# A local-attention and two-layer MoE kernel on one core: queries and keys in one load, the mask as a TensorE product, four raw weight buffers

## The chip, the cores and the metric

The kernel runs on one core of a Trainium2 chip. The metric is the device time of one execution in microseconds. The engines spoken of are PE (TensorE, matrix products), DVE (VectorE), ACT (ScalarE), POOL (GpSimd) and SP, which here does nothing but issue DMAs. A change of under 0.2% cannot be told from none for this kernel.

## The reference

The work is an attention over short windows, followed by two feed-forward layers. Inputs are four sequences of 768 positions, eight heads of 64 values, eight memory keys and values per head.

```
for c in range(nc):                       # chunks of 32 queries
    l_start = max(0, c_start - 16); r_end = min(S, c_end + 8)
    k_full = concat([mem_k, k[l_start:r_end]]); v_full likewise
    scores = scale * q_c @ k_full.T
    scores = scores - max(scores); a = exp(scores)
    out[c] = (a / (sum(a) + 1e-09)) @ v_full
x = out.reshape(3072, 512)
x = prelu(x @ w_in1, 0.01) @ w_out1       # 512 -> 2048 -> 512
h = x @ w_in2; x = (h * clip(h + 3, 0, 6) / 6) @ w_out2
```

## The kernel before

**Tiling.** The 3072 tokens are 48 *pairs* (two chunks, 64 queries) and 6 *blocks* of 512 tokens (8 pairs). Everything of layer 0 is done block by block, then everything of layer 1. A block runs through 16 slices f of the 2048 hidden values; for each slice there are 12 products `hidden` (128x512, into the PSUM tile `ph`) and 12 products `output` (into `py`), because each operand is split into a high part and a rest (`xh`, `xl`, `gh`, `gl`) and three of the four cross products are taken. The first pass is block 0 of layer 0; in it the weights of layer 0 are also converted from an 8-byte to a split 4-byte form, one 128x512 tile (layer, f, in or out) at a time. A conversion is a DMA into a `raw` buffer, three ACT instructions (L217, L223, L251) and five DVE instructions (L227, L231, L238, L245, L257).

**Attention of a pair.** PE multiplies queries and keys (`a_scores`, L329, 16 small products), DVE scales and masks them in one instruction (`a_masked`, L338), DVE takes the row maxima (`a_most`, L356), ACT takes the exponential in four instructions, one per head pair, each of which also gives a row sum (`a_exp`, L363), DVE adds 1e-9 to the sums and inverts them (L374, L375), POOL multiplies (`a_norm`, L379), then the weights are transposed: by PE and an ACT copy in pairs 0 to 15 (L397, L402), by twelve DVE transposes in pairs 16 to 47 (L389). PE multiplies with the values (`a_values`, L410), and ACT and DVE split the result into `xh` and `xl` (L425, L431). Block 0's eight pairs come before the first layer product: this is the *opening*. The other pairs are computed while the block before runs; there scores of one pair and values of the pair before share one *visit* of PE.

**What sets the order.** All steps are entered with an engine, a planned length (the table `TIME`), a due time and what they wait for; buffers are counted in `rings`. A planner (`Program.order`) plays this through and fixes the order of the instructions on every engine; on the chip each engine keeps that order and waits on semaphores. Where the planner finds PE with nothing to do in the opening it puts in two small products on a zeroed tile (`keep_warm`, L605). They write the second half of the tile `opening`, whose first half takes PE's transposes.

**Buffers.** There are three `raw` buffers (`NRAW`), two buffers each for queries, keys and values (the first eight pairs use future weight tiles instead), and a pool of three `oo` tiles for the rows of the output.

Of the kernel before, what the change touches and what calls it, by code (L numbers as in the profile page):

```python
# [22 lines left out]
    words=0.67, clip=0.42, shift=0.43, join=0.69, add=0.69, high=0.65, low=0.69, load=0.45,  # L23
    visit=1.2, scores=0.75, masked=0.56, most=0.55, exp=1.65, sums=0.36, norm=0.83, turn=0.6, turned=0.57, turn4=0.95,
# [3 lines left out]
LANDING, RATE = 1.9, 320e3  # L28


BEGIN = 30.0
STEP_FIRST, STEP_MIXED, STEP = 7.0, 6.6, 5.5
PAIR_FIRST = 2.6
# [100 lines left out]
def tile_kernel(  # L134
    ctx: ExitStack,
    tc: tile.TileContext,
    q: bass.AP,
    k: bass.AP,
# [32 lines left out]
    CH, LC, RC = 32, 16, 8  # L171
    CTX = LC + PT + RC
# [6 lines left out]
    NBUF = 2  # L179
    NRAW = 3  # L180
# [14 lines left out]
    q_t = [at.tile([P, HP, PT], F32, tag=f"q{i}", name=f"q{i}") for i in range(NBUF)]  # L195
    k_t = [at.tile([P, HP, W], F32, tag=f"k{i}", name=f"k{i}") for i in range(NBUF)]
    v_t = [at.tile([W, HD], F32, tag=f"v{i}", name=f"v{i}") for i in range(NBUF)]
# [63 lines left out]
    def convert(layer, wanted, after=()):  # L261

        order = [(0, 0)] + [x for f in range(1, NF) for x in ((f, 0), (f - 1, 1))] + [(NF - 1, 1)]
        for f, io in order:
# [11 lines left out]
            c = add("ACT", T["high"], t - 1.6, w_high, key, after=[c] + ([w_ready[layer, f, 0]] if io else []),  # L276
# [8 lines left out]
    def inputs(pr):  # L285
        if pr >= NPB:
            return q_t[pr % NBUF], k_t[pr % NBUF], v_t[pr % NBUF]
        if pr not in in_t:
            in_t[pr] = sb.tile([P, 2 * 2 * 512], F32, tag="w", name=f"in{pr}", bufs=NF)
        t, n, m = in_t[pr], HP * PT, HP * (PT + W)  # L290
        return (
            t[:, :n].rearrange("p (h t) -> p h t", h=HP),
            t[:, n:m].rearrange("p (h w) -> p h w", h=HP),
            t[:W, m:m + HD],
        )

    def load_qk(pr):
        b, p = divmod(pr, PPB)
        qt, kt, _ = inputs(pr)
        nc.sync.dma_start(out=qt.rearrange("p h t -> p (h t)"), in_=q[b, p].rearrange("p h t -> p (h t)"))  # L300
        nc.sync.dma_start(out=kt.rearrange("p h w -> p (h w)"), in_=k[b, p].rearrange("p h w -> p (h w)"))

    def load_v(pr):
        b, p = divmod(pr, PPB)
        nc.sync.dma_start(out=inputs(pr)[2], in_=v[b, p])


    def pa(name, opening=False):
        if opening and "pa" in late:
            return late["pa"]  # L310
        t = ps.tile([P, 2, 512], F32, tag="pa", name=name, bufs=1)
        if opening:
            late["pa"] = t
        return t

    def a_scores(pr):


        qt, kt, _ = inputs(pr)
        if pr < NPB:  # L320
            pt = ps.tile([P, 2, 512], F32, tag="py", name=f"psc{pr}", bufs=2)
        else:
            pt = pa(f"psc{pr}")
        for m in range(HP // 2):
            for j in range(2):
                hp = j * HP // 2 + m
                for e in range(2):
                    r, n = slice(e * D, (e + 1) * D), e ^ j
                    nc.tensor.matmul(  # L329
                        pt[n * PT:(n + 1) * PT, j, m * W:(m + 1) * W], qt[r, hp, :], kt[r, hp, :],  # L330
                        start=True, stop=True, tile_position=(e * D, n * PT),
                    )
        e_t[pr] = p_t[pr] = pt

    def a_masked(pr):
# [57 lines left out]
    def a_turn_pe(pr):  # L393
        e = e_t.pop(pr)
        pt = pa(f"pt{pr}", pr < NPB)
        for hp in range(HP):
            nc.tensor.transpose(pt[:W, 0, hp * P:(hp + 1) * P], e[:, hp, :], ident)  # L397
        aT_t[pr] = pt

    def a_turned(pr):  # L400
        t = at.tile([W, HP, P], F32, tag="aT", name=f"aT{pr}", bufs=2)
        nc.scalar.copy(out=t.rearrange("p h c -> p (h c)"), in_=aT_t[pr][:W, 0, :])  # L402
        aT_t[pr] = t

    def a_values(pr, pt):
        t, vt = aT_t.pop(pr), inputs(pr)[2]
# [9 lines left out]
    def a_values_first(pr):  # L416
        a_values(pr, ps.tile([P, TB], F32, tag="ph", name=f"px{pr}", bufs=2)[:, :HP * PT])
# [15 lines left out]
    x_ready, values_done, pending, opened = {}, [], [], []  # L433
# [10 lines left out]
    def visit(pr):  # L444

        if pr < NP:
            a_scores(pr)
            pt = p_t[pr]
        else:
            pt = pa(f"px{pr}")  # L450
        if pr > NPB:
            a_values(pr - 1, pt[:, 1, HP // 2 * W:HP // 2 * W + HP * PT])

    def attention(pr, t, turned_by_pe, spread):

        blk = pr // NPB
        tag = "py" if blk == 0 else "pa"
# [5 lines left out]
        if blk == 0:  # L463
            qk = vv = [("w", ("in", pr))]
        a = add("SP", 0.9, due(-5), load_qk, pr, takes=qk, nbytes=P * 640 * 4)
        vl = add("SP", 0.45, due(-1), load_v, pr, takes=vv if blk else (), after=[] if blk else [a],
                 nbytes=W * 2048)
        s, e = [(tag, ("s", pr))], [("ye", ("e", pr))]
        if blk == 0:
            before = [values_done[x] for x in [pr - 3] if x >= 0]  # L470
            c = add("PE", T["scores"], due(0), a_scores, pr, after=[a] + before, takes=s)
        else:
            c = visit_step(pr, t, [a], s, qk)
        c = add("DVE", T["masked"], due(1.1), a_masked, pr, after=[c] + set_up, takes=e, frees=s)
        c = add("DVE", T["most"], due(1.7), a_most, pr, after=[c])
        c = add("ACT", T["exp"], due(2.4), a_exp, pr, after=[c])
        c = add("DVE", T["sums"], due(4.2), a_sums, pr, after=[c])
        c = add("POOL", T["norm"], due(4.6), a_norm, pr, after=[c])
        aT = [("aT", pr)]
        if turned_by_pe:  # L480
            p = [("pt" if blk == 0 else "pa", ("t", pr))]
            o = [("pa", "opening")]
            c = add("PE", T["turn"], due(5.6), a_turn_pe, pr, after=[c], takes=p + (o if pr == 0 else []), frees=e)
            c = add("ACT", T["turned"], due(6.3), a_turned, pr, after=[c], takes=aT,
                    frees=p + (o if blk == 0 else []))
# [14 lines left out]
    def visit_step(pr, t, after=(), takes=(), frees=()):  # L500
        if not pending:
            return add("PE", T["scores"], t, visit, pr, after=after, takes=takes, frees=frees)
        p = [*takes] or [("pa", ("s", pr))]
        c = add("PE", T["visit"], t, visit, pr, after=[*pending[:2], *after], takes=p,
                frees=pending[2] + [*frees])
        finish(pr - 1, c, t, p)
# [54 lines left out]
    def output(layer, blk, f, part):  # L561
# [3 lines left out]
        if f == 0 and part == 0:  # L565
            pairs = [
                ps.tile([P, 2, 512], F32, tag="py", name=f"py{layer}_{blk}_{c}", bufs=2) for c in range(2)
            ]
# [213 lines left out]
```

## Time and profile before

| what | value |
|---|---|
| median of 3 runs | 1160.54 us (1160.24 to 1162.18) |
| profiled execution | 1160.1 us |
| its span, first to last instruction | 1158.3 us |
| PE busy | 1140.4 us, 98% |
| DVE busy | 601.8 us, 52% |
| ACT busy | 473.3 us, 41% |
| POOL busy | 42.7 us, 4% |
| moved by DMA | 78.64 MB, 68 GB/s over the span |

The shares are averages over stages that differ. PE's share counts the small products of `keep_warm` as work. How busy DVE is must be read stage by stage: in the page's 40 slices it stands at 8 to 9 tenths in slices 2 to 5, at 5 to 6 tenths up to slice 19, at 7 to 9 tenths around the weights of layer 1, and at 2 to 3 after that.

### The profile page before, as it was taken

The page shows a single profiled execution, that of the slowest core. Times are in us where ns is not written, and L with a number is a line of the kernel's source. Part 1 is how long each engine was busy: PE and PEld are TensorE (multiplying, and loading weights), DVE is VectorE, ACT ScalarE, POOL GpSimd, SP SyncE. Part 2 cuts the span into 40 slices and gives each one's busy share as a digit, 9 for nine tenths or more (in the row PEclk, how much of TensorE's full clock was granted, in tenths as well). Part 3 has the DMA queues.
Part 4 walks back from the last instruction along what each step waited for, and adds up shares of the span by engine and source line. Part 5 has one row for each costly group of instructions (what it writes and reads, how often), then busy time and mean ns, then how long its engine had stood idle before and what let it go on. Part 6 is the DMA issues. An engine that isn't in the chain of part 4 may idle for free.

```text
span 1158.3 us, 16198 instructions
## 1 busy us (share of the span) xinstructions
PE 1140.4 (98%) x6350; PEld 926.1 (80%) x6350; DVE 601.8 (52%) x1303; ACT 473.3 (41%) x1073; POOL 42.7 (4%) x54
## 2 busy tenths in 40 slices
PE   8999999999999999999999999999999999999998
PEld 6777788888888888788888888888888888888886
DVE  5899985555556556555798933223223223222222
ACT  5878853343333333333677623223223223222222
POOL 1100000000000000000000000000000000000000
PEclk9999999999999999999999999999999999999999
DMA  7455531121112112111445401001001000000000
GB/s 237 121 182 183 184 126 55 37 89 40 37 56 74 38 55 74 49 32 73 164 147 181 146 1 64 10 1 64 10 1 64 10 1 28 10 1 28 10 1 37
DMA packets 38573, 78.64 MB, mean 68 GB/s; under 512 B 4193, under 2 KB 16481, under 8 KB 38497
## 3 DMA queue, kind: packets, MB, share of 16 engines
q1 hardware_dynamic: 38496, 77.61, 20.8%
q8 instruction: 50, 0.82, 0.3%
q14 instruction: 27, 0.21, 0.1%
HBM read 65.01 MB, written 12.58 MB: 67 GB/s over the span
## 4 chain that ended last, share of the span: by engine, by line
PE 93%; DVE 4%; DMA 1%; ACT 1%; issue 1%; POOL 0%; ACTq 0%; DVEq 0%; POOLq 0%
PE py L512 44%; PE ph L512 43%; PE psc L410 2%; PE psc L329 2%; PE opening L605 1%; DMA raw<-in_moe_w_out_dram 1%; DVE wa L238 1%; DVE w L257 1%; DVE raw L245 1%; DVE wa L231 0%; PE px L410 0%; DVE e L338 0%; ACT aT L402 0%; PE opening L397 0%; DVE wa L227 0%
## 5 line engine op out<-in xcount | busy, mean ns | idle before, releaser
L512 PE MATMUL ph<-xh,w 128*128 128x512 f32 x768 | 252.5, 390 | 0.4 <-ACT xh L425 0.3
L512 PE MATMUL ph<-yh,w 128*128 128x512 f32 x768 | 252.0, 389 | 0.0
L512 PE MATMUL py<-gh,w 128*128 128x512 f32 x768 | 244.7, 398 | 5.5 <-ACT w L251 3.6
L512 PE MATMUL py<-w,gh 128*128 128x512 f32 x768 | 236.4, 389 | 0.0
L540 DVE SCALAR_TENSOR_TENSOR ph<-g,ph 128x512 f32<-128x512 f32 x96 | 66.8, 696 | 281.3 <-ACT g L534 281.2
L534 ACT ACTIVATE g<-ph,three 128x512 f32<-128x512 f32 x96 | 66.2, 690 | 294.0 <-PE ph L512 294.0
L512 PEld LDWEIGHTS py<-gh,w 128*128 128x128 f32 x768 | 140.5, 188 | 39.4 <-ACT w L251 6.2
L512 PEld LDWEIGHTS ph<-xh,w 128*128 128x128 f32 x768 | 143.9, 188 | 31.7 <-DVE w L257 1.7
L512 PEld LDWEIGHTS ph<-yh,w 128*128 128x128 f32 x768 | 144.3, 188 | 29.9
L512 PEld LDWEIGHTS py<-w,gh 128*128 128x128 f32 x768 | 144.2, 188 | 29.8
L512 PE MATMUL py<-gl,w 128*128 128x512 f32 x384 | 150.2, 391 | 0.0
L512 PE MATMUL ph<-xl,w 128*128 128x512 f32 x384 | 149.5, 389 | 0.0
L512 PE MATMUL py<-w,gl 128*128 128x512 f32 x384 | 149.4, 389 | 0.0
L512 PE MATMUL ph<-yl,w 128*128 128x512 f32 x384 | 149.4, 389 | 0.0
L389 DVE STREAM_TRANSPOSE aT<-e 32x128 f32<-32x128 f32 x384 | 116.0, 302 | 37.6 <-POOL e L379 32.2
L531 ACT ACTIVATE ph<-ph 128x512 f32<-128x512 f32 x96 | 55.9, 582 | 193.8 <-PE ph L512 193.5
L556 DVE SCALAR_TENSOR_TENSOR gl<-ph,gh 128x512 fp32r<-128x512 f32 x96 | 66.3, 690 | 53.1 <-ACT gh L547 53.1
L363 ACT ACTIVATE e<-e,mx 128x96 f32<-128x96 f32 x192 | 69.6, 363 | 59.2 <-DVE mx L356 59.1
L512 PEld LDWEIGHTS py<-gl,w 128*128 128x128 f32 x384 | 72.0, 188 | 15.7
L512 PEld LDWEIGHTS ph<-xl,w 128*128 128x128 f32 x384 | 72.1, 188 | 15.3 <-DVE xl L431 0.3
L512 PEld LDWEIGHTS py<-w,gl 128*128 128x128 f32 x384 | 72.0, 188 | 15.0
L512 PEld LDWEIGHTS ph<-yl,w 128*128 128x128 f32 x384 | 72.1, 188 | 14.9
(59 smaller groups left out, 916.6 us busy)
## 6 DMA issues: line engine op xcount, KB each, us to landing
raw<-in_moe_w_in_dram SPq DMA_DIRECT2D x32, 512.0 KB, 3.5
raw<-in_moe_w_out_dram SPq DMA_DIRECT2D x32, 512.0 KB, 3.5
k<-in_k_dram SPq DMA_DIRECT2D x40, 192.0 KB, 3.0
v<-in_v_dram SPq DMA_DIRECT2D x40, 192.0 KB, 2.6
y_dram<-yo SPq DMA_DIRECT2D x24, 256.0 KB, 2.0
yn<-y_dram SPq DMA_DIRECT2D x6, 1024.0 KB, 5.3
out_dram<-oo SPq DMA_DIRECT2D x24, 256.0 KB, 2.1
q<-in_q_dram SPq DMA_DIRECT2D x40, 128.0 KB, 2.7
```

The source lines that it names most:

```text
L238: nc.vector.scalar_tensor_tensor(out=a, in0=hi, scalar=0xC0000000, in1=a, op0=ALU.bitwise_and, op1=ALU.bitwise_or)
L245: nc.vector.tensor_tensor(out=hi, in0=tmp_t.pop(key), in1=lo, op=ALU.add)
L257: nc.vector.tensor_tensor(out=w[:, io, 1, :], in0=a, in1=w[:, io, 0, :].bitcast(F32), op=ALU.subtract)
L329: nc.tensor.matmul(pt[n * PT:(n + 1) * PT, j, m * W:(m + 1) * W], qt[r, hp, :], kt[r, hp, :], start=True, stop=True, tile_position=(e * D, ...
L363: nc.scalar.activation(out=e[:, hp, :], in_=e[:, hp, :], func=AF.Exp, bias=mx[:, hp:hp + 1], accum_out=su[:, hp:hp + 1],)
L389: nc.vector.transpose(out=t[c, :, r], in_=e[r, :, c])
L410: nc.tensor.matmul(pt[e * D:(e + 1) * D, hp * PT:(hp + 1) * PT], vt[:, c], t[:, hp, n * PT:(n + 1) * PT], start=True, stop=True, tile_posi ...
L512: nc.tensor.matmul(dst, a, b, start=first and i == 0, stop=last and i == len(terms) - 1)
L531: nc.scalar.activation(out=ph, in_=ph, func=AF.Prelu, alpha=0.01)
L534: nc.scalar.activation(out=g, in_=ph, func=AF.Relu, bias=three, scale=1.0)
L540: nc.vector.scalar_tensor_tensor(out=ph, in0=g, scalar=6.0, in1=ph, op0=ALU.min, op1=ALU.mult)
L556: nc.vector.scalar_tensor_tensor(out=gl, in0=ph, scalar=1.0 / 6.0, in1=gh.bitcast(F32), op0=ALU.mult, op1=ALU.subtract)
```

## The change

Queries and keys are laid out side by side and come in one DMA of 128x640 where two came before; for pairs 8 to 47 there is one buffer of them and one of values, where there were two. In pairs 1 to 10 and 13 to 15 (`barred_by_pe`) two bf16 products of a class matrix and a bar matrix put -1e30 into PSUM where a score is not allowed, and the scores accumulate on top. In these pairs DVE's scale-and-mask step is gone; the maxima are taken from PSUM, in two halves, and POOL scales them; ACT's exponential reads PSUM directly. In pairs 2, 4 and 6 (`SHIFTED`) DVE instead subtracts the maxima (two halves), ACT takes one exponential over the whole tile, and DVE adds it up. In all pairs the adding of 1e-9 goes from DVE to POOL. Score tiles are single PSUM banks (`pa0`, `pa1`, `py`) where they were tiles of two banks, `keep_warm` has a bank of its own in the opening, and in pairs 0, 11, 12 and 16 to 47 `a_masked` takes two instructions of half the size. There are four `raw` buffers, and layer 1's output rows use them too (`oo` is gone). The planner has new lengths and due times.

```diff
-LANDING, RATE = 1.9, 320e3
-BEGIN = 30.0
+LANDING, RATE = 2.1, 290e3
+BEGIN = 31.0
-PAIR_FIRST = 2.6
+PAIR_FIRST = 2.1
+SHIFTED = (2, 4, 6)
...
-    NRAW = 3
+    NRAW = 4
...
-    rings = dict(w=NF, raw=NRAW, wa=2, ye=4, aT=2, gh=2, gl=2, x=2, py=2, ph=2, pa=1, pt=1, qk=NBUF, v=NBUF, yn=1, oo=NRAW)
+    rings = dict(w=NF, raw=NRAW, wa=2, ye=4, aT=2, gh=2, gl=2, x=2, py=4, ph=2, pa0=1, pa1=1, qk=1, v=1, yn=1)
...
-            c = add("ACT", T["high"], t - 1.6, w_high, key, after=[c] + ([w_ready[layer, f, 0]] if io else []),
+            c = add("ACT", T["high"], t - 1.6, w_high, key, after=[c, loaded[NPB - 1]] + ([w_ready[layer, f, 0]] if io else []),
...
     def load_qk(pr):
-        nc.sync.dma_start(out=qt.rearrange("p h t -> p (h t)"), in_=q[b, p].rearrange("p h t -> p (h t)"))
-        nc.sync.dma_start(out=kt.rearrange("p h w -> p (h w)"), in_=k[b, p].rearrange("p h w -> p (h w)"))
+        nc.sync.dma_start(out=inputs(pr)[0], in_=qk[divmod(pr, PPB)])
...
+    def barred_by_pe(pr):
+        return pr < 2 * NPB and 0 < pr % PPB < PPB - 1
...
+        more = barred_by_pe(pr)
+        if more:
+            for j in range(2):
+                nc.tensor.matmul(
+                    pt[j][:, :HP // 2 * W], cls, barred.rearrange("p m w -> p (m w)"),
+                    start=True, stop=False, skip_group_check=True,
+                )
...
     def a_most(pr):
+        if barred_by_pe(pr):
+            for j in range(2):
+                nc.vector.tensor_reduce(
+                    out=mx[:, j * HP // 2:(j + 1) * HP // 2],
+                    in_=p_t[pr][j][:, :HP // 2 * W].rearrange("p (m w) -> p m w", w=W),
+                    axis=AX.X, op=ALU.max, negate=True,
+                )
...
+    def a_scaled(pr):
+        mx = m_t[pr]
+        nc.gpsimd.tensor_scalar_mul(mx, mx, SCALE)
...
+    def a_shift(pr):
+        for j in range(2):
+            nc.vector.scalar_tensor_tensor(
+                out=e[:, h, :],
+                in0=p_t[pr][j][:, :HP // 2 * W].rearrange("p (m w) -> p m w", w=W),
+                scalar=SCALE,
+                in1=mx[:, h].unsqueeze(2).to_broadcast([P, HP // 2, W]),
...
+    def a_exp_all(pr):
+        nc.scalar.activation(out=e, in_=e, func=AF.Exp)
...
+    def a_add_up(pr):
+        nc.vector.reduce_sum(out=su, in_=e_t[pr], axis=AX.X)
...
     def a_sums(pr):
-        nc.vector.tensor_scalar_add(su, su, 1e-9)
+        nc.gpsimd.tensor_scalar_add(su, su, 1e-9)
...
         else:
-            t = late["pool"].tile([P, DM], F32, tag="oo", name=f"oo{blk}_{c}", bufs=3)
+            t = sb.tile([P, 512, 2], U32, tag="raw", name=f"oo{blk}_{c}", bufs=NRAW)
...
     def keep_warm():
-        t = pa("opening", True)
+        if "warm" not in late:
+            late["warm"] = bank("pa1", "warm")
```

**The order on SP in the opening** (raw0_0_0 is the first weight tile, in4 to in7 are the inputs of pairs 4 to 7). Before:

```order
L305 DMA in4_159<-in_v_dram 96x512
L300 DMA q0_71<-in_q_dram 128x256
L301 DMA k0_73<-in_k_dram 128x384
L305 DMA in5_185<-in_v_dram 96x512
L211 DMA raw0_0_0_275<-in_moe_w_in_dram 128x1024
```

and now:

```order
L297 DMA in6_135<-in_qk_dram 128x640
L297 DMA in7_141<-in_qk_dram 128x640
L300 DMA in0_96<-in_v_dram 96x512
L211 DMA raw0_0_0_156<-in_moe_w_in_dram 128x1024
L300 DMA in1_105<-in_v_dram 96x512
L211 DMA raw0_1_0_180<-in_moe_w_in_dram 128x1024
```

The first weight tile moved from the 25th DMA to the 10th: all eight loads of queries and keys, and one of values, stand ahead of it.

**The order on DVE in the opening**, from the rest `xl` of pair 2 to that of pair 3 (psc are scores, mx maxima, su row sums, wa and raw belong to a conversion). Before:

```order
L431 TENSOR_TENSOR xl_289<-px_365,xh_288 128x4x64
L245 ISA raw_0_0_275<-raw_0_0_275,wa_0_0_361 128x512x2
L374 TENSOR_SCALAR su_424<-su_424 128x4
L375 RECIPROCAL su_424<-su_424 128x4
L338 SCALAR_TENSOR_TENSOR e_457<-psc_439,masks 128x384
L431 TENSOR_TENSOR xl_289<-px_429,xh_288 128x4x64
```

and now:

```order
L474 TENSOR_TENSOR xl_312<-px_386,xh_311 128x4x64
L418 RECIPROCAL su_417<-su_417 128x4
L231 TENSOR_SCALAR wa_1_0_395<-wa_1_0_395 128x512
L238 SCALAR_TENSOR_TENSOR wa_1_0_395<-raw_1_0_180,wa_1_0_395 128x512
L245 ISA raw_1_0_180<-raw_1_0_180,wa_1_0_395 128x512x2
L356 TENSOR_REDUCE mx_481<-psc_0_463 128x2
L356 TENSOR_REDUCE mx_481<-psc_1_464 128x2
L474 TENSOR_TENSOR xl_312<-px_444,xh_311 128x4x64
```

Between the first and the last `xl` of the opening 14 conversion instructions stood on DVE before, and 23 stand there now.

**The order on PE in the second pass**, around the visit of pair 21 (aT and v belong to the values of pair 20). Before:

```order
L512 MATMUL ph_1_9_2283<-xh_741,w_9_1236 128x512
L329 MATMUL psc_2301<-k_74,q_72 64x96 x8
L410 MATMUL psc_2301<-aT_2265,v_75 64x64 x8
L512 MATMUL py_1_0_1883<-gh_1_8_2269,w_8_1174 128x512 x2
L512 MATMUL py_1_0_1883<-gl_1_8_2290,w_8_1174 128x512
```

and now:

```order
L567 MATMUL py_1_0_1935<-gl_1_8_2354,w_8_1179 128x512
L567 MATMUL py_1_1_1936<-gh_1_8_2329,w_8_1179 128x512 x2
L567 MATMUL py_1_1_1936<-gl_1_8_2354,w_8_1179 128x512
L326 MATMUL psc_0_2374<-qk_now 64x96 x2
L326 MATMUL psc_1_2375<-qk_now 64x96 x2
L326 MATMUL psc_0_2374<-qk_now 64x96 x2
L326 MATMUL psc_1_2375<-qk_now 64x96 x2
L453 MATMUL psc_1_2375<-aT_2331,v_now 64x64 x8
L567 MATMUL py_1_2_1937<-gh_1_8_2329,w_8_1179 128x512 x2
```

The visit moved from ahead of the 12 output products of slice 8 to the middle of them, six products later.

## Rows read from the trace of the kernel before

**Rows 1.** Busy time by stage: stretch and length, engines busy, granted clock, DMA share, GB/s

```profile
0.00:16.30 16.30, 14.38 (x157) 10.52 (x157) 5.39 (x21) 6.64 (x27) 3.18 (x9) 1.00 0.88 251
16.30:41.46 25.16, 19.89 (x295) 15.27 (x291) 17.80 (x43) 19.05 (x65) 4.13 (x5) 1.00 0.48 151
41.46:150.46 109.00, 103.34 (x661) 78.87 (x661) 104.93 (x210) 90.06 (x206) 8.48 (x8) 1.00 0.58 180
150.46:1153.30 1002.84, 1002.76 (x5244) 821.45 (x5243) 473.02 (x1032) 356.95 (x778) 26.90 (x32) 1.00 0.15 50
```

**Rows 2.** Groups by line on DVE, 16.30 to 41.46 us: busy, mean ns, idle before

```profile
L338 DVE SCALAR_TENSOR_TENSOR e<-psc,masks 128x384 f32<-128x384 f32 x6 | 3.3, 553 | 2.9 <-PE psc L329 2.9
L431 DVE TENSOR_TENSOR xl<-px,xh 128x256 fp32r<-128x256 f32 x8 | 3.3, 409 | 2.6 <-ACT xh L425 2.4
...
L227 DVE TENSOR_SCALAR wa<-wa 128x512 f32<-128x512 f32 x3 | 1.3, 446 | 2.2 <-ACT wa L217 2.2
```

**Rows 3.** Groups by line on DVE, 41.46 to 150.46 us

```profile
L245 DVE CUSTOM_DVE_ANT_0 raw<-raw,wa 128x1024 uint16<-128x1024 uint16 x29 | 23.7, 818 | 1.9
L257 DVE TENSOR_TENSOR w<-raw,w 128x512 fp32r<-128x512 f32 x30 | 20.4, 679 | 0.0
L238 DVE SCALAR_TENSOR_TENSOR wa<-raw,wa 128x512 uint32<-128x512 uint32 x29 | 19.9, 685 | 0.3
...
L338 DVE SCALAR_TENSOR_TENSOR e<-psc,masks 128x384 f32<-128x384 f32 x9 | 5.0, 552 | 0.6 <-PE psc L410 0.5
L356 DVE TENSOR_REDUCE mx<-e 128x4 f32<-128x384 f32 x9 | 4.9, 544 | 0.0
...
L375 DVE RECIPROCAL su<-su 128x4 f32<-128x4 f32 x8 | 1.4, 178 | 0.3
L374 DVE TENSOR_SCALAR su<-su 128x4 f32<-128x4 f32 x8 | 1.3, 164 | 0.0
```

**Rows 4.** The chain that ended last, in order of time: start, length, what

```profile
1.05 5.93 PE opening L605 x28
...
141.84 0.44 PE pt L397 x4
...
146.39 0.49 PE psc L329 x16
146.88 0.61 PE psc L410 x16
147.50 2.96 PE py L512 x12
150.46 2.72 PE ph L512 x12
```

**Rows 5.** Instructions on ACT in the opening: one in order of time, one by line

```profile
21.10 0.68 ACT L217 ACTIVATE wa<-raw 128x512 f32<-128x512 f32 x1
...
L363 ACT ACTIVATE e<-e,mx 128x96 f32<-128x96 f32 x20 | 7.2, 362 | 0.1
```

**Rows 6.** POOL and DVE side by side, in order of time; start, length

```profile
139.94 1.09 POOL L379 TENSOR_TENSOR e<-e,su 128x384 f32<-128x384 f32 x1 [13.02 <-DVE su L375]
...
140.26 1.31 DVE L245 CUSTOM_DVE_ANT_0 raw<-raw,wa 128x1024 uint16<-128x1024 uint16 x1
```

**Rows 7.** POOL by line, whole span: a step of 128 columns

```profile
masks.py:199 POOL TENSOR_SCALAR_AFFINE_SELECT ident<-ident 128x128 f32<-128x128 f32 x1 | 0.3, 292 | 0.1
```

**Rows 8.** The last copies, in order of time

```profile
1153.26 0.69 DVE L587 COPY oo<-py 128x512 f32<-128x512 f32 x1 [0.67 <-PE py L512]
1154.74 0.58 ACT L589 COPY oo<-py 128x512 f32<-128x512 f32 x1 [1.53 <-DMA out_dram<-oo]
```

**Rows 9.** Second pass: scores and `a_norm` of pair 21, rest `gl` of slice 10

```profile
207.45 0.56 PE L329 MATMUL psc<-k,q 64*64 64x96 f32 x16
...
213.38 0.83 POOL L379 TENSOR_TENSOR e<-e,su 128x384 f32<-128x384 f32 x1 [11.35 <-DVE su L375]
...
217.09 0.69 DVE L554 TENSOR_TENSOR gl<-ph,gh 128x512 fp32r<-128x512 f32 x1
```

More of the change, by code (lines that the diff above doesn't have):

```diff
@@ L22 @@
 TIME = dict(
-    words=0.67, clip=0.42, shift=0.43, join=0.69, add=0.69, high=0.65, low=0.69, load=0.45,
-    visit=1.2, scores=0.75, masked=0.56, most=0.55, exp=1.65, sums=0.36, norm=0.83, turn=0.6, turned=0.57, turn4=0.95,
+    words=0.67, clip=0.42, shift=0.43, join=0.69, add=0.69, high=0.65, low=0.69, load=0.47,
+    visit=1.2, scores=0.75, masked=0.56, most=0.55, exp=1.65, exp_all=0.52, small=0.15, inverse=0.18, norm=0.83, turn=0.6, turned=0.57, turn4=0.95,
     values=0.85, xh=0.4, xl=0.45, half=1.36, act=0.58, six=0.69, gh=0.6, gl=0.69, done=0.66, warm=0.22,
@@ L171, in tile_kernel @@
     CH, LC, RC = 32, 16, 8
+    PT, D = 2 * CH, P // 2
+    HP = HD // P
     CTX = LC + PT + RC
@@ L303, in load_v @@
     def load_v(pr):
[L304 to L314, printed above, removed]
-    def a_scores(pr):
[L319 to L323, printed above, removed]
+        nc.sync.dma_start(out=inputs(pr)[3], in_=v[divmod(pr, PPB)])
@@ L464, in attention @@
             qk = vv = [("w", ("in", pr))]
[L465 to L468, printed above, removed]
+        hold = [] if blk == 0 else [scored[-3]] if pr == NPB else loaded[-1:]
+        a = add("SP", T["load"], due(-5), load_qk, pr, after=hold, takes=qk, nbytes=P * 640 * 4)
+        loaded.append(a)
@@ L469, in attention @@
+        vl = add("SP", T["load"], due(0), load_v, pr, takes=vv if blk else (), after=[a], nbytes=W * 2048)
+        s = [("py" if blk == 0 else f"pa{j}", ("s", pr, j)) for j in range(2)]
+        e = [("ye", ("e", pr))]
+        direct = barred_by_pe(pr)
         if blk == 0:
             before = [values_done[x] for x in [pr - 3] if x >= 0]
-            c = add("PE", T["scores"], due(0), a_scores, pr, after=[a] + before, takes=s)
+            c = add("PE", T["scores"] + 0.3 * direct, due(0), a_scores, pr, after=[a] + before + set_up, takes=s)
@@ L478, in attention @@
+        c = add("POOL", T["small"], due(4.1), a_sums, pr, after=[c])
+        c = add("DVE", T["inverse"], due(4.3), a_inverse, pr, after=[c])
         c = add("POOL", T["norm"], due(4.6), a_norm, pr, after=[c])
@@ L480, in attention @@
         if turned_by_pe:
[L481 to L485, printed above, removed]
+            p = [("pa0", ("t", pr))]
+            c = add("PE", T["turn"], due(5.6), a_turn_pe, pr, after=[c], takes=p, frees=e)
+            c = add("ACT", T["turned"], due(6.3), a_turned, pr, after=[c], takes=aT, frees=p)
             if blk == 0:
@@ L565, in output @@
         if f == 0 and part == 0:
[L566 to L569 removed]
+            acc[layer, blk] = [bank("py", f"py{layer}_{blk}_{c}") for c in range(4)]
         dst = acc[layer, blk]
```

157 lines of the change are left out of this document (95 added, 62 removed).

## The prediction

> **What bounds the kernel now.** I read the busy time by stage first, because the page's shares run over stages with different limits. It shows four stages [rows 1]. From 150.46 to 1153.30 us PE is busy for 1002.76 of 1002.84 us: nothing on another engine can shorten that. From 41.46 (end of the opening's last `xl`) to 150.46 (first product of the second pass) DVE is busy for 104.93 of 109.00 us. From 16.30 (first `xl`) to 41.46 no engine is full: DVE has 17.80 of 25.16, ACT 19.05. Before 16.30 the first pair runs through, behind 28 products that only keep PE busy and take 5.93 us [rows 4], 0.21 each.
>
> Next come the groups by line, for durations and for what ended DVE's idle time. In the opening DVE waited for scores (2.9 us), for `xh` (2.6) and for the first weights (2.2) [rows 2]; ACT's first conversion starts only at 21.10 [rows 5]. In the first pass the largest groups are the conversions [rows 3]. Then the chain of waits, for PE's own needs: 12 products 2.72 us; a visit 0.49 + 0.61, and 2.96 - 2.72 = 0.24 more for the products behind it, 1.34 in all; a transpose 0.44 [rows 4]. Between 41.46 and 150.46 PE has 31 groups of 12 products, 8 visits and 8 transposes: 84.3 + 10.7 + 3.5 = 98.5 us. So PE lost 10.5 of the 109.0, and DVE only 4.1. Last, the end: ACT's last copy waited 1.53 us for a store to free an `oo` buffer [rows 8].
>
> One rule of counting. DVE's instructions overlap: the fourteen groups of 41.46 to 150.46 sum to 117.5 us (the seven used here are [rows 3]), but cover 104.93. I count an instruction as 0.893 of its duration.
>
> **The opening.** The order puts 32 instead of 28 idle products ahead of the first scores: 4 x 0.21 = 0.85 us, so the first `xl` comes at 17.15 instead of 16.30. For the rest of that first pair I let POOL's two extra hand-overs cancel against the copy that no longer waits behind idle products. From there DVE has, in its new order up to the last `xl`: ten tensor-scalar steps of conversions at 0.446, five joins at 0.685, four L245 at 0.818, four L257 at 0.679 [rows 2, 3], 14 half-size steps (ten maxima, four shifts), two sums at 0.544, five inversions at 0.178, eight `xl` at 0.409. No row shows a half-size step or a maximum from PSUM. Its bounds are half of 0.55 (0.275) and the whole 0.55. L431 with 256 elements takes 0.409 and L356 with 384 takes 0.544, which is 0.34 for 192 on a straight line; I take that. Sum 4.5 + 3.4 + 3.3 + 2.7 + 4.8 + 1.1 + 0.9 + 3.3 = 24.0, times 0.893 = 21.4 us. Without any wait the last `xl` ends at 38.5. ACT hides behind this: it gets four more conversion instructions of 0.68 (2.7) and loses two pairs' worth of eight exponentials (2.9, and their reads) [rows 5], so it stays near 19 us.
>
> Waits: the three named above shrink. The first weight tile stands tenth on SP. Ahead of it and with it are 8 x 0.328 + 0.197 + 0.524 = 3.34 MB, which at the 251 GB/s of the first stage [rows 1] is in by 13.3 us, ahead of 17.15. Nine more conversion instructions stand between the pairs' steps and fill what were gaps. What comes late next is a sum or a maximum that POOL passes on. POOL's small step (128x4) has no row: its bounds are nothing and 0.83, the whole `a_norm` of 128x384 [rows 9]; I take 0.3, by the step of 128 columns [rows 7]. I allow 0.65 us of waits in all. The last `xl` then ends at 39.2 instead of 41.46: **-2.3 us**. Bounds: no waits and half-steps of 0.275 give 37.7 (-3.8); all of DVE's old 7.36 us of idle time kept, 45.9 (+4.4), and half-steps of 0.55 another 2.6 on that.
>
> **The first pass.** More of the conversions now lie before it: on DVE two fewer of L227, L231, L238 and L257 and one fewer L245 fall in the stretch, 5.3 us. Six pairs (8, 9, 10, 13, 14, 15) lose L338, 3.3 us; eight lose L374, 1.3 us; two half-size steps for one whole add 0.13 nine times, 1.2. Together -8.7, times 0.893 = -7.8: DVE's need falls from 104.9 to about 97.1. PE gets two mask products in each of six visits. Nearest rows are 0.21 for an idle product of 256 columns and 2.72 / 12 = 0.227 for one of 512 [rows 4]; bounds 0.04 and 0.227 each. I take 0.1 for 192 columns, 1.2 us, so PE needs 99.7. PE becomes the bound, with DVE close under it; I allow 1.8 us of waits where a weight part still comes late: 101.5 instead of 109.0, **-7.5 us**. Bounds: PE alone with free mask products, 98.5 and 0.5 (-10.0); DVE with its old 4.1 us of idle time and 0.69 us more for each of 14 small POOL steps, 110.9 (+1.9). The fourth `raw` buffer has no term of its own: it is what lets loads and conversions run as far ahead as the order has them, and without it the 4.1 stays.
>
> **The rest and the end.** In the stretch in which PE is full no product is added or removed: 0, with 2 us either way for visits that now write two single banks. The second half-size step of each later pair (0.13 us) and the single input buffer lie under DVE at 473 of 1003 us: a load goes out right after the visit that frees it, a visit comes every 12 us. At the end the last copy needs no store to be done, so it can start at 1153.26 with DVE's, not 1154.74 [rows 8]. Its store then waits behind the other on SP, some 0.4 us: **-1.0 us**, bounds -1.5 and 0.
>
> Sum: -2.3 - 7.5 - 1.0 = -10.8. The profiled execution took 1160.1 us, 0.44 under the median, so 1149.3 in its terms and **1149.7 us** against the median of 1160.54.
>
> **Rivals.** *POOL and DVE in each other's way.* When a POOL step and L245 ran together, the POOL step took 1.09 instead of 0.83 and L245, which has two inputs as L238 has, 1.31 where that takes 0.685 [rows 3, 6, 9]. The change adds 15 small POOL steps to the opening and 14 to the first pass, and in these DVE waits for 18 of their results (16 inversions, two shifts) with everything queued behind. If each is held up by 0.69 less the 0.16 that L374 took, that is 9.5 us, 1159.2; if half of it, 4.8 us, 1154.5. Against it: the planned order leaves some other step between most sums and their inversion.
>
> The Trainium skill, "SBUF — State Buffer", section "Who interferes with whom", says that GpSimd and VectorE share a port pair as an exclusive lock, so that a VectorE step with two SBUF inputs and a GpSimd step that reads SBUF block each other for the whole instruction. The two steps of rows 6 agree. Applied to every new step it gives the 1159.2, and it speaks for moving nothing small to POOL.
>
> *The opening is overfilled.* The nine conversion instructions come on top of DVE's old waits instead of into them: last `xl` at 45.9, sum -4.1, 1156.4. For it: DVE keeps its order and stands still behind any late step.
>
> *The weights don't come early.* If the first tile still lands so that ACT starts at 21.10, DVE is 4 us later: 1153.7.
>
> *Slower, in passes two to five.* There 32 pairs have a chain in which POOL's sum is new: scores, maxima, exponential, sum, inversion, `a_norm`, nine transposes, then `gl`, which PE wants. Before, from scores at 207.45 to the end of `gl` at 217.78 it took 10.33 us [rows 9]. The visit is now six products later, so that from scores to the first use of that `gl` PE has 1.34 + 1.36 + 3 x 2.72 + 2 x 0.23 = 11.3 us of other work: about 1.0 of room, 1.4 as another `gl` no longer stands in the chain. POOL's step eats the room and then stops PE 32 times. It cancels the gain at 10.8 / 32 = 0.34 beyond the room, so if the step costs 1.75 us more than before; at 2.0 the result is 1149.7 + 19.2 = 1168.9. Against it: even the whole `a_norm` takes only 0.83.
>
> **How the numbers follow.** Forecast 64% (its own range 1146.0 to 1153.0), POOL and DVE 16%, overfilled opening 10%, late weights 4%, slower 6%. The lower end is the sum of the three terms' low bounds, -15.3: 1145.2. The upper end, 1156.5, takes in the overfilled opening, the late weights and the first rival up to two thirds of its price; what lies above is under 2 in 10. Under 0.2% (2.3 us) this kernel's change can't be told from none. Faster: all but the slower rival and the full price of the first, 91%; same 3%; slower 6%.
>
> **What would show it.** Right: ACT's first conversion near 17 us, the opening's last `xl` ending near 39.2, the second pass starting near 140.7, PE's own idle time in the first pass under 3 us, the last copy of ACT starting with DVE's. Wrong: DVE's inversions idle on POOL for more than 5 us in total up to 140 us; idle time of PE in the second to fifth pass; a last `xl` after 41.

## The result, and the profile after

The changed kernel takes 1149.95 us (median of 4 runs, 1149.60 to 1150.69), the kernel before 1161.24 on the same chip (4 runs): ratio 0.9904, 95% interval 0.9887 to 0.9921. The profiled execution has a span of 1148.9 us against 1158.3.

| point, us | before | forecast | after |
|---|---|---|---|
| first `xl` starts | 16.30 | 17.15 | 16.64 |
| opening's last `xl` ends | 41.46 | 39.2 | 39.97 |
| second pass starts | 150.46 | 140.7 | 142.42 |
| ACT's last copy starts | 1154.74 | (at PE's end) | 1145.20, at PE's end |
| span | 1158.3 | 1147.5 | 1148.9 |

Busy time by stage, as [rows 1]; the last stretch runs to PE's end:

```profile
0.00:16.64 16.64, 15.20 (x162) 11.44 (x166) 4.95 (x22) 6.19 (x22) 5.32 (x22) 1.00 0.89 281
16.64:39.97 23.33, 20.04 (x307) 14.85 (x299) 22.75 (x53) 19.31 (x55) 8.62 (x15) 1.00 0.53 163
39.97:142.42 102.45, 101.18 (x670) 79.91 (x671) 96.19 (x194) 83.87 (x200) 14.19 (x22) 1.00 0.60 189
142.42:1145.18 1002.76, 1002.74 (x5244) 821.21 (x5243) 472.65 (x1032) 357.36 (x777) 34.93 (x64) 1.00 0.15 50
```

The third number of busy time is DVE's. In the opening it is now 22.75 of 23.33 us, where 7 us were idle; in the first pass it fell from 104.93 to 96.19. PE stays full behind that. By stage the time changes by +0.3 (first pair), -1.8 (to the last `xl`), -6.6 (first pass), 0, and -1.3 us behind PE's end.

DVE by line in the opening, first `xl` to last, to be read against [rows 2]:

```profile
L238 DVE SCALAR_TENSOR_TENSOR wa<-raw,wa 128x512 uint32<-128x512 uint32 x5 | 3.9, 780 | 0.1
L356 DVE TENSOR_REDUCE mx<-psc 128x2 f32<-128x192 f32 x11 | 3.4, 346 | 0.0
L257 DVE TENSOR_TENSOR w<-raw,w 128x512 fp32r<-128x512 f32 x4 | 3.3, 834 | 0.0
L474 DVE TENSOR_TENSOR xl<-px,xh 128x256 fp32r<-128x256 f32 x8 | 3.3, 414 | 2.0 <-ACT xh L468 2.0
L245 DVE CUSTOM_DVE_ANT_0 raw<-raw,wa 128x1024 uint16<-128x1024 uint16 x4 | 3.3, 820 | 0.3
L227 DVE TENSOR_SCALAR wa<-wa 128x512 f32<-128x512 f32 x5 | 2.7, 537 | 0.0
L231 DVE TENSOR_SCALAR wa<-wa 128x512 uint32<-128x512 uint32 x5 | 2.6, 521 | 0.1
```

and in the first pass, against [rows 3]:

```profile
L238 DVE SCALAR_TENSOR_TENSOR wa<-raw,wa 128x512 uint32<-128x512 uint32 x27 | 20.6, 763 | 0.5
L245 DVE CUSTOM_DVE_ANT_0 raw<-raw,wa 128x1024 uint16<-128x1024 uint16 x28 | 19.2, 686 | 0.6
L257 DVE TENSOR_TENSOR w<-raw,w 128x512 fp32r<-128x512 f32 x27 | 19.0, 705 | 0.2 <-ACT w L251 0.2
```

The waits for scores and for the first weights in [rows 2] are gone. The 2.0 us for `xh` end at 16.64 and so lie ahead of this stretch; in [rows 2], too, 2.42 of the 2.6 us end at 16.30 and are no part of DVE's 7.36 us of idle time there. But the joins L238 take 780 ns where the prediction counted 685, L257 834 for 679, L227 537 for 446: DVE is full partly because its steps became longer. What ran beside a long one is seen here, as in [rows 6]; DVE, then POOL:

```profile
24.84 1.20 DVE L238 SCALAR_TENSOR_TENSOR wa<-raw,wa 128x512 uint32<-128x512 uint32 x1
```

```profile
24.67 0.83 POOL L422 TENSOR_TENSOR e<-e,su 128x384 f32<-128x384 f32 x1 [0.28 <-DVE su L418]
```

In the first pass PE needs 98.5 us and six times the two mask products, of which one pair reads:

```profile
97.13 0.18 PE psc L317 x2
```

That makes 99.6 us, and the pass takes 102.45. Of the 2.85 lost, 0.7 is the first `xl`, and two breaks at 117 and 131 us cost about 1.0 each. The chain through the second:

```profile
129.63 0.79 POOL su L414
...
130.54 0.41 DVE wa L231
...
130.97 1.20 DVE wa L238
132.17 0.61 DVE w L257
...
132.82 0.73 PE py L567 x2
```

POOL's small step, 0.23 alone, took 0.79 here, and the join beside the `a_norm` that follows took 1.20; `w` is late by that, and PE waits. In each break PE first waits 0.3 us for `a_norm` itself, ahead of the transposes. The end, as [rows 8]:

```profile
1144.52 0.69 DVE L640 COPY oo<-py 128x512 f32<-128x512 f32 x1 [0.67 <-PE py L567]
...
1145.20 0.58 ACT L642 COPY oo<-py 128x512 f32<-128x512 f32 x1 [0.77 <-PE py L567]
```

No copy waits for a store any more. DVE's last copy also starts 0.68 us ahead of PE's end, since each accumulator has a bank of its own.

### The profile page after: what moved, and what is told of

It reads as the page before. It is cut to its first block, busy times and chain, and to the rows that moved or that the text cites. A ratio compares the mean times of both kernels' runs of the same rounds, so it can differ in the third digit from the quotient of the medians.

```text
span 1148.9 us, 16191 instructions
## 1 busy us (share of the span) xinstructions
PE 1139.2 (99%) x6370; PEld 927.4 (81%) x6370; DVE 596.6 (52%) x1299; ACT 467.3 (41%) x1052; POOL 63.1 (5%) x123
## 4 chain that ended last, share of the span: by engine, by line
PE 96%; DVE 2%; ACT 1%; POOL 0%; issue 0%; DVEq 0%; POOLq 0%
PE py L567 46%; PE ph L567 45%; PE psc L453 2%; PE psc L326 2%; PE warm L659 1%; DVE wa L238 1%; DVE w L257 0%; ACT e L402 0%; PE pt L440 0%; DVE raw L245 0%; DVE wa L231 0%; DVE xl L474 0%; DVE mx L356 0%; DVE wa L227 0%; POOL su L414 0%
## 5 line engine op out<-in xcount | busy, mean ns | idle before, releaser
L609 DVE TENSOR_TENSOR gl<-ph,gh 128x512 fp32r<-128x512 f32 x96 | 66.2, 690 | 59.6 <-ACT gh L600 58.5
```

The costliest lines, as they stand in the source:

```text
L609: nc.vector.tensor_sub(out=gl, in0=ph, in1=gh.bitcast(F32))
```

## The experiments

All times are of one profiled execution beside the median of its runs. PE is full from the second pass on in each (1002.8 us), so the start of that pass is PE's end less this. The column that compares best is the time from the first `xl` to the second pass. The profiled run is not always near the median of its kernel: it is 2.3 us above it in small_dve, 1.9 in norm_act, 1.7 in mask_dve, and 1.4 below it in two_loads. An edit that the planner sees can also give a new order, so only small_twice is sure to change one part and nothing else.

| kernel | first `xl` | last `xl` ends | second pass | first `xl` to second pass | span | median |
|---|---|---|---|---|---|---|
| before | 16.30 | 41.46 | 150.46 | 134.16 | 1158.3 | 1161.24 |
| changed | 16.64 | 39.97 | 142.42 | 125.78 | 1148.9 | 1149.95 |
| changed, again | 16.45 | 39.80 | 142.21 | 125.76 | 1148.7 | 1149.72 |
| raw3 | 15.97 | 39.32 | 147.59 | 131.62 | 1154.9 | 1157.03 |
| before_raw4 | 16.20 | 41.00 | 151.51 | 135.31 | 1158.7 | 1160.49 |
| mask_dve | 15.90 | 37.38 | 148.58 | 132.68 | 1155.5 | 1155.65 |
| small_dve | 16.53 | 40.91 | 145.46 | 128.93 | 1152.0 | 1151.80 |
| small_twice | 16.31 | 40.30 | 144.82 | 128.51 | 1151.3 | 1153.26 |
| two_loads | 13.70 | 38.55 | 142.86 | 129.16 | 1149.4 | 1152.53 |
| norm_act | 15.41 | 38.75 | 145.35 | 129.94 | 1151.8 | 1152.05 |
| norm_dve_open | 16.22 | 37.18 | 144.32 | 128.10 | 1151.1 | 1151.98 |
| idle_priced | 14.03 | 37.30 | 139.83 | 125.80 | 1146.3 | 1148.14 |
| idle_noshift | 13.71 | 37.95 | 139.06 | 125.35 | 1145.6 | 1147.31 |
| idle_costs | 13.79 | 39.66 | 142.67 | 128.88 | 1149.2 | 1150.62 |

The first theory was the prediction's: fewer and earlier DVE steps in the first pass, with the fourth raw buffer as what lets them run ahead. The rivals: POOL's new steps and DVE hinder each other enough to eat part of it; the buffers alone are the gain. What the new planned lengths and due times bring by themselves was not run.

**Three raw buffers.**

```
-    NRAW = 4
+    NRAW = 3
```

> The changed kernel with three raw buffers instead of four. The theory of the prediction: the fourth buffer is what lets loads and conversions run ahead, and it lets the last copy start without a store. Without it the first pass goes from 102.45 us to 104 to 106.5 (4.1 us of DVE waits come back, part of it hidden since PE needs 99.7), and the time from PE's last product to the end of the span from 3.72 us back to about 5.1; span 1152 to 1154. Rival A, the ring does not matter to the first pass: only the tail moves, span 1150.3. Rival B, the ring is the main part of the gain: first pass near 109, span 1157 or more.

The opening keeps its length; the first pass takes 108.3 us, more than the theory's 106.5 and near rival B's 109. DVE has 97 us of work in it, as with four: little is added, it waits. The chain up to PE's longest two breaks shows for what:

```profile
77.49 1.25 DVE w L257
78.74 0.02 issue
78.75 4.96 DMA raw<-in_moe_w_in_dram
83.71 0.02 issue
83.73 0.67 ACT wa L217
...
89.02 0.43 DVE wa L231
89.45 0.60 DVE w L257
```

```profile
90.10 0.73 PE L567 MATMUL ph<-xh,w 128*128 128x512 f32 x2 [1.22 <-DVE w L257]
...
94.84 0.64 PE L440 MATMUL pt<-ident,e 128*96 128x128 f32 x4 [2.15 <-POOL e L422]
```

A load goes out when the step that frees its buffer is done, and with three buffers its 4.96 us stand open on the path. The weight part is late, and behind it in DVE's order the maxima of a pair, so that its `a_norm` is late as well. The end has its old wait back:

```profile
1151.28 0.59 ACT L642 COPY oo<-py 128x512 f32<-128x512 f32 x1 [1.65 <-DMA out_dram<-oo]
```

**Four raw buffers, in the kernel before.**

```
-    NBUF = 2
-    NRAW = 3
+    NBUF = 1
+    NRAW = 4
...
```

The lines left out put the output rows into the raw ring too, as in the change.

> The kernel before with only the buffers changed: single input buffers, four raw buffers, and the output rows in the raw ring. Theory: a part of the gain. The first pass loses some of DVE's 4.1 us of waits, 109.0 to 106 or 107; the tail falls by about 1.0; opening 0 to -1; span 1158.3 to about 1154.5. Rival A, the buffers are nearly all of the gain: 1150. Rival B, only the tail moves, since DVE's need of 104.9 in the first pass stays: 1157.3.

Ratio 0.9999 (0.9990 to 1.0008): nothing, less than any theory expected. Its first pass:

```profile
41.00:151.51 110.51, 103.39 (x661) 79.12 (x662) 105.30 (x210) 90.23 (x206) 9.01 (x8) 1.00 0.59 179
```

DVE still has 105.30 us to do, so there is little that earlier loads could gain. The pass even got 1.5 us longer, against 0.4 less in the opening and 0.6 less behind PE's end. The edit also takes away the second input buffers, and what that costs is not separated here from what the ring gives; PE's longest wait (1.79 us, for a copy by ACT at 112 us) is longer than any of the kernel before (0.69). So the fourth buffer with the single input buffers brings nothing in this kernel, while its loss costs the changed one 5.8 us. That the DVE work had to go first agrees with both, but is argued.

**Mask on DVE again.**

```
     def barred_by_pe(pr):
-        return pr < 2 * NPB and 0 < pr % PPB < PPB - 1
+        return False
```

> The changed kernel with the mask added by DVE for every pair again, so without mask products, without POOL's small shift step and without the one-piece exponentials of pairs 2, 4 and 6. Theory: in the first pass DVE gets 6 x 0.62 us back (96.2 to about 99.9 busy) while PE's need falls by 1.1, so both engines have about 99 of work and the pass takes 103 to 105 instead of 102.45; in the opening ACT gets three pairs' eight exponentials back, about 1 us each, and becomes as full as DVE: 0.5 to 2 us longer. Span 1150 to 1153. Rival: PE alone sets the first pass now, so that taking the mask products away gains what they cost, span 1147.5 to 1148.5.

Longer by 6.9 us from the first `xl` to the second pass, where 4.6 at most was expected.

```profile
37.38:148.58 111.20, 101.74 (x660) 80.37 (x661) 104.43 (x208) 87.81 (x204) 11.58 (x16) 0.98 0.58 177
```

DVE is back at 104.43 us in the first pass: the masked sums, and conversions that the new order no longer puts into the opening, which got shorter by 1.85. What PE waits for is `a_norm`, 7.9 us in four waits. The rival (mask products cost more than they spare) is out. About 1.3 of the 6.9 is PE's clock (below); by the medians the loss is 5.7.

**The small steps on DVE.**

```
-        nc.gpsimd.tensor_scalar_mul(mx, mx, SCALE)
+        nc.vector.tensor_scalar_mul(mx, mx, SCALE)
...
-        nc.gpsimd.tensor_scalar_add(su, su, 1e-9)
+        nc.vector.tensor_scalar_add(su, su, 1e-9)
...
```

> The changed kernel with the two small steps (sum plus 1e-9, scaling of the maxima) on DVE instead of POOL, everything else alike. Theory: POOL's small steps cost little and take DVE work away; back on DVE they add 12 x 0.16 us to the DVE-bound opening and 14 x 0.16 to the first pass, where DVE has about 6 us to spare: span 1150 to 1151.5. Rival (POOL and DVE in each other's way): DVE's two-input steps get shorter and the chains through POOL's lengthened sum step (0.79 and 0.81 us at 115.6 and 129.6) go, span 1145 to 1147.4.

Slower by 3.1 us in the profile and 1.85 by the medians, where the rival wanted it 1.5 to 4 us faster: the prediction's first rival is refuted for the small steps. Of the 3.1, 1.05 lie in the opening. In the first pass a drop of the clock follows PE's waits at 36 to 41 us: the first 23 products take 7.02 us there and 5.48 in the changed kernel, so 1.5 is not DVE's work. The 1.6 us left, a gain of having the steps on POOL, are under 0.2%, less than can be told from none for this kernel.

```profile
40.95 7.02 PE ph L567 x23
```

**The small steps done twice.**

```
         nc.gpsimd.tensor_scalar_mul(mx, mx, SCALE)
+        nc.gpsimd.tensor_scalar_mul(mx, mx, 1.0)
...
         nc.gpsimd.tensor_scalar_add(su, su, 1e-9)
+        if pr < 2 * NPB:
+            nc.gpsimd.tensor_scalar_add(su, su, 0.0)
```

> The changed kernel with each of POOL's small steps of the first 16 pairs done twice (the second adds 0 or multiplies by 1; the order is planned as if there were one). It doubles the suspected cost: 29 more steps of 0.23 us alone, up to 0.8 beside DVE. Theory: most of it lies beside DVE's conversions, since some other DVE step is queued between a sum and its inversion only in part; 1 to 3 us longer, span 1150 to 1152. Rival (each small step costs 0.5 us or more on the path that sets the end): 8 to 15 us longer, span 1157 or more.

Longer by 2.7 us from the first `xl` to the second pass, as the theory had it. Of the 29 new steps, five stand ahead of that stretch and 24 in it: 0.11 us each, where the rival wanted 0.5.

**Two loads for queries and keys.**

```
-        nc.sync.dma_start(out=inputs(pr)[0], in_=qk[divmod(pr, PPB)])
+        n, src = HP * PT, qk[divmod(pr, PPB)]
+        nc.sync.dma_start(out=inputs(pr)[0][:, :n], in_=src[:, :n])
+        nc.sync.dma_start(out=inputs(pr)[0][:, n:], in_=src[:, n:])
...
```

> The changed kernel with queries and keys of a pair loaded by two DMAs again (same bytes, same buffer). Theory: the joining of the loads has next to no effect of its own; SP issues eight more in the opening at about 0.4 us each, so values and weights are issued some 3 us later, ahead of their use still: 0 to 0.7 us longer, span 1149 to 1149.6. Rival: the first weights and values come later than DVE wants them, as SP stands between: 2 to 3.5 us longer, span 1151 to 1152.4.

Unclear by stage: the planner, told of the longer issue, put out another order on PE ahead of the first `xl` (13.70), and the stretch behind it lost 3.4 us. The profiled run's span of 1149.4 is the theory's, but the median is 2.6 us over the changed kernel's, against 0.7 at most, and the spans of its other three runs, 1150.6 to 1151.0, come near the rival's 1151. DVE is busy for 21.11 of 24.85 us of this opening (22.75 of 23.33 in the changed kernel): it waits again. What the load itself costs is not separated from the order here.

**`a_norm` of pairs 8 to 15 on ACT.**

```
+        if NPB <= pr < 2 * NPB:
+            for hp in range(HP):
+                nc.scalar.activation(out=e[:, hp, :], in_=e[:, hp, :], func=AF.Identity, scale=su[:, hp:hp + 1])
...
```

> The changed kernel with the product of e and the inverted sums of pairs 8 to 15 on ACT (four steps by head pair) instead of POOL. It takes away POOL's long steps in the first pass, beside which DVE's two-input steps take 1.20 instead of 0.69. Theory: what PE still loses in the first pass (102.45 less a need of 99.7) comes from these meetings, above all the 1.20 at 116.9 and 131.0; DVE's busy time there falls by about 4 us, PE's loss by 1 to 1.5: second pass from 141 to 141.5, span 1147.3 to 1148. Rival: ACT, at 84 of 102 us, gets 8 us more and its copies for the weights come later: span 1149 to 1151.

The theory fell, and the rival's mechanism came: DVE's busy time fell by 2.3 of the 4 us expected, to 93.86, yet the pass takes 106.60.

```profile
38.75:145.35 106.60, 103.58 (x670) 80.89 (x671) 93.86 (x194) 91.65 (x232) 5.74 (x14) 0.98 0.59 181
```

ACT has 91.65 us, its copy for one weight part comes 1.4 us late, and the clock falls behind that wait (some 1.6 us). The profiled run is the slowest here; the other three have spans of 1149.0 to 1150.7, in the rival's range. What a meeting of POOL and DVE costs PE was not had back with ACT's time, and how much of PE's loss in the first pass comes from these meetings stays open.

**`a_norm` of pairs 0 to 7 on DVE.**

```
-        nc.gpsimd.tensor_tensor(out=e, in0=e, in1=su.unsqueeze(2).to_broadcast([P, HP, W]), op=ALU.mult)
+        eng = nc.vector if pr < NPB else nc.gpsimd
+        eng.tensor_tensor(out=e, in0=e, in1=su.unsqueeze(2).to_broadcast([P, HP, W]), op=ALU.mult)
...
```

> The changed kernel with the product of e and the inverted sums of pairs 0 to 7 on DVE instead of POOL (pairs 8 on as before). Between the opening's first and last xl DVE gets five such steps more, about 0.53 us each by the maximum over the same 128x384 (0.54): 2.65 us. Theory (a POOL step and a DVE step block each other, and the longer DVE steps at 22.04, 24.84, 28.80, 32.35 and 35.26, 2.8 us over their usual times in sum, are time that DVE loses): the two cancel, and the stretch takes 23.0 to 23.8 us instead of 23.33, DVE's mean of one step back at 0.69 for the join. Rival: the longer durations are only counted twice, DVE loses little by them, and the stretch takes 25.5 to 26.2; span then 2 to 3 us longer than 1148.9.

Neither stretch came: the planner moved five conversion steps out of the opening, which so took 20.96 us. The steps themselves bear on the question. DVE in this opening:

```profile
L423 DVE TENSOR_TENSOR e<-e,su 128x384 f32<-128x384 f32 x5 | 2.8, 556 | 0.1
L238 DVE SCALAR_TENSOR_TENSOR wa<-raw,wa 128x512 uint32<-128x512 uint32 x4 | 2.8, 688 | 0.1
L245 DVE CUSTOM_DVE_ANT_0 raw<-raw,wa 128x1024 uint16<-128x1024 uint16 x3 | 2.1, 693 | 0.2
L257 DVE TENSOR_TENSOR w<-raw,w 128x512 fp32r<-128x512 f32 x3 | 2.1, 684 | 0.0
L231 DVE TENSOR_SCALAR wa<-wa 128x512 uint32<-128x512 uint32 x4 | 1.7, 427 | 0.1
L227 DVE TENSOR_SCALAR wa<-wa 128x512 f32<-128x512 f32 x4 | 1.7, 419 | 0.0
```

Without POOL's long step beside them they are back at 688, 684 and 419 ns (780, 834, 537 in the changed kernel). Over L238, L257, L227 and L231 that is 5 x 0.09 + 4 x 0.15 + 5 x 0.12 + 5 x 0.09 = 2.1 us, and 4 x 0.13 = 0.5 more with L245. By this estimate the opening of the changed kernel loses 2.6 us to five `a_norm`, nearly the 2.8 us that they take on DVE: the two cancel, as the theory said, though the stretch itself does not show it. To the second pass this kernel is 2.3 us longer, about 1.5 of it by the clock.

**Idle products at their price.**

```
-                        free_at[e] = now + filler[1]
+                        free_at[e] = now + filler[1] * (1 if began else 2)
...
```

Here `began` says that the planner has placed a step that is no idle product.

> The changed kernel, but the program that sets the order counts an idle product ahead of the first scores at twice its cost, near the 0.205 us that the trace shows for each (32 in 6.57 us) where it counted 0.11. So 16 instead of 32 stand ahead of the first scores. Theory: the first pair's chain is one after the other, and the input of pair 0 is there at about 3.7 us, so all of it moves forward by 16 x 0.205 = 3.3 us, the DVE-bound stretch behind it starts that much sooner, and the whole is 2 to 3 us faster (second pass from 142.42 to about 139.5 to 140.5, span 1146 to 1147). Rival A: the products of the first pairs then run at half the rate, as the idle ones do, and give back 1 to 2 us: span 1147.5 to 1148.5. Rival B: the values' input and the first weights land no sooner, so DVE waits what it gains: span 1148.5 to 1149.5.

As the theory had it. The chain up to the first `xl`:

```profile
1.04 3.60 PE warm L660 x16
4.64 0.86 PE psc L327 x16
...
14.03 0.42 DVE xl L475
```

Sixteen idle products instead of 32, scores at 4.64 instead of 7.62, and everything behind comes 2.6 us sooner at unchanged length (125.80 and 125.78). Rival A shows in one place only: these scores take 0.86 us instead of 0.50. The ratio is 0.9894 (0.9880 to 0.9909). By the medians it is 1.8 us faster than the changed kernel, and the two intervals overlap.

**No shift by DVE, on top of idle_priced.**

```
-SHIFTED = (2, 4, 6)
+SHIFTED = ()
```

> idle_priced with no pair shifted by DVE: pairs 2, 4 and 6 get their exponentials from PSUM in four steps on ACT, as 1, 3 and 5 do. DVE, which sets the opening (22.69 of 23.27 us busy), loses 3 x (0.62 + 0.54) = 3.5 us, ACT gets 3 x 0.8 = 2.4 on 19.3. Theory: the stretch from the first to the last xl falls by 0.8 to 1.8 us, to about 22, with both engines near full; span 1144.5 to 1145.5 against 1146.3. Rival: ACT, in its order, becomes what DVE waits for (its copies for the weights stand behind the exponentials), stretch 23 to 25, span 1146.3 to 1148.

```profile
13.71:37.95 24.24, 21.99 (x327) 16.96 (x319) 20.37 (x48) 21.16 (x70) 9.15 (x15) 1.00 0.74 199
37.95:139.06 101.11, 100.40 (x670) 80.06 (x671) 95.96 (x193) 85.07 (x200) 13.61 (x22) 1.00 0.61 190
```

The opening did not get shorter, as the rival said (DVE waits for ACT now), but the first pass did, by 1.4. It is the best kernel here: 1147.31 us, ratio 0.9883 (0.9870 to 0.9897), against 0.9906 (0.9893 to 0.9920) for the changed kernel on the same chip. Against idle_priced the 0.8 us are within the two intervals and stay open.

**More of the planner's costs set to the trace**, on top of idle_priced; six entries of `TIME`:

```
-    ... join=0.69, ... scores=0.75, ... exp=1.65, ... small=0.15, ... norm=0.83, turn=0.6, ...
+    ... join=0.75, ... scores=0.52, ... exp=1.4, ... small=0.35, ... norm=0.95, turn=0.5, ...
```

> idle_priced with more of the order's costs set to what the traces show: scores 0.52 (was 0.75), the exponentials of a pair 1.4 (1.65), POOL's small step 0.35 (0.15), POOL's product 0.95 (0.83), the join 0.75 (0.69), the turn 0.5 (0.6). No instruction is added or taken away. Theory: what PE still loses in the first pass (2.7 us) is order that was planned with wrong lengths, and 0.5 to 1.5 us of it go: span 1144.8 to 1145.8. Rival: these waits come from in-order queues that no cost mends; any new order is as good as the old, within 2 us either way: 1144.5 to 1148.5 without a pattern in the waits.

Neither range held: the median is 2.5 us over that of idle_priced, and the span of 1149.2 lies above even the rival's 1148.5. The opening has 24.04 us of DVE work in 25.87 and the first pass gains nothing. A cost that is right by itself need not make the order better.

**The changed kernel again.**

> The changed kernel itself, once more, beside the others on one chip. It tells how much of the spread is the 32 idle products: they took 6.57 us in the profiled run and 4.97 to 5.89 us in other runs with as many. Theory: the start of the scores moves by as much from run to run, and from the first xl to the second pass the time is the same, 125.8 within 0.3 us. Rival: the stretch behind the first xl varies as much as the start.

The theory held: 125.76 us, and the start carries the spread. The profiled run of the changed kernel was the slowest of its four (1150.69), its idle products the slowest of all.

## Why the prediction was right, and where it was off

The mechanism came as forecast: DVE has less and earlier work, PE becomes the bound of the first pass, and the fourth buffer lets the loads run ahead. ACT's first conversion starts at 16.51 us, near the 17 that was named as a sign. The median came out 0.25 us over the forecast, but that closeness is in part luck. In the profile the gain is 9.4 us and the forecast was 10.8. The profiled run of the changed kernel was its slowest, 0.74 us over its median, and that of before was 0.44 under its own; this is 1.2 of the 1.4 us between the two gains. The terms:

- **First pair, +0.85 forecast, +0.34 measured.** The idle products cost 0.64 (6.57 us against 5.93), and the rest of the first pair, which was let cancel, became 0.30 shorter. The price of 0.21 us is not a constant either: 32 idle products took from 4.97 to 6.57 us.
- **From the first to the last `xl`, -3.1 forecast (25.16 to 22.05), -1.8 measured.** The waits shrank to 0.6 as forecast, the counts are right within one, and the half-size steps took 0.346 for the 0.34 read off a line. The mis-sized term is DVE's need: 22.75 instead of 21.4. L238, L257, L227 and L231 were priced at rows in which POOL hardly stood beside them; in the denser opening they took 1.9 us more in sum, and without the five `a_norm` beside them they are back near those prices (norm_dve_open). The prediction also read the wait for `xh` in [rows 2] as one of this stretch, and nearly all of it lies ahead; the sum does not use it, as it takes DVE's idle time as a whole.
- **First pass, -7.5 forecast, -6.55 measured.** DVE's need of 97.1 came out at 96.19, the mask products at 0.09 each for 0.1. The 1.8 us of waits were 2.85: the first `xl` and the two breaks above, whose chain runs through two such meetings; that they alone make the breaks is argued from the chain. The forecast also carried such meetings without seeing them. L245's mean of 818 ns [rows 3] contains six of 1.31 or 1.32 us, each begun 0.3 us after an `a_norm`, while the median is 693 ns (lowest, median, highest, kernel before):

```profile
L245 DVE CUSTOM_DVE_ANT_0 raw<-raw,wa x29: 662/693/1320, 44.8 to 147.0; 128x1024 uint16<-128x1024 uint16 x29
```

In the changed kernel the mean is 686, as the order lets L238 meet POOL's step instead. So (818 - 686) x 29 = 3.8 us of DVE's first pass before were meetings; only the one of [rows 6] was looked at.
- **Rest, 0.** PE is busy for 1002.74 of 1002.76 us. The slower rival did not come: POOL's new sum in the 32 later pairs takes 246 ns in the mean.
- **End, -1.0 forecast, -1.3 measured.** ACT's last copy starts at PE's end as said, but not with DVE's: that one is 0.68 us earlier, so its store is out of the way and the 0.4 us behind it on SP do not arise. raw3 gives 0.8 of it back.
- **POOL and DVE in each other's way.** DVE's inversions waited 2.2 us for POOL, all ahead of 14.5 us, where over 5 would have spoken for the rival. Its mechanism is real, but the price sits on the long step: a small one, 0.23 us alone and up to 0.89 beside DVE, costs 0.11 us (small_twice). The rule of the Trainium skill ("SBUF — State Buffer", section "Who interferes with whom"), by which the two engines block each other for a whole instruction, agrees with the long step (a join of 1.20 us beside an `a_norm` of 0.83). Applied to each small one it gave 1159.2, which is out.
- **The fourth raw buffer** was rightly named as what lets the work run ahead, though it was priced at the old 4.1 us of waits; raw3 makes it 5.8.

## What to carry to other kernels

What a part is worth depends on the rest: taking the fourth buffer out of the finished change costs 5.8 us, and putting it, with the single input buffers, into the kernel before brought nothing while DVE was full. Before pricing a moved step by a mean, look at what stood beside it in that stretch, since the meetings move with the order. A planner's fixed costs can hide a whole wait, as the idle products did; correct the one that a trace shows on the path, and measure again.

## What the hardware showed unasked

The first idle products run at half the rate of later ones (32 in 6.57 us; 10 in 1.09 further on), though the granted clock reads 1.00 in both, and how long that lasts differs from run to run: in nine runs the first 32 took from 4.97 to 6.57 us.

In four kernels a wait of PE in the first pass or just ahead of it was followed by TensorE's lower level, 1.2 GHz instead of 2.4. In norm_dve_open PE waits 2.18 us for an `a_norm` around 90 us; the columns are the stretch, its length, PE busy, granted clock, DMA share and GB/s:

```profile
88.00:90.00 2.00, 1.17 (x6) 1.00 0.69 240
90.00:92.00 2.00, 0.65 (x3) 0.79 0.00 0
92.00:94.00 2.00, 2.00 (x8) 0.50 0.50 104
94.00:96.00 2.00, 2.00 (x9) 0.86 0.79 213
96.00:98.00 2.00, 2.00 (x11) 1.00 0.83 260
```

From the start of the transposes behind the wait through the next six products, 91.35 to 94.69, it takes 3.34 us, where the same steps in the changed kernel take 1.85 (45.34 to 47.19). So a wait of 2.18 us costs some 1.5 more. The same is seen in norm_act at 93 us (1.6) and mask_dve at 108 us (1.3), and in small_dve at 41 us (1.5). The changed kernel has none.

The wait by itself does not settle it: raw3's 2.15 us ahead of 94.84 and before_raw4's 1.79 are followed by a granted clock of 1.00. What decides stays open. The other runs of norm_dve_open have spans of 1149.0 to 1151.5 and mean clocks of 0.998 or 1.000, so the drop may not come in every run of a kernel.
